# Attention with strided heads first and local heads in turn, expert 0 in three equal token groups, and its first low halves on GpSimd

## The chip, the cores and the metric

The program runs on one core of a Trainium2 chip. The metric is device time in microseconds (us) of one execution; lower is better. The engines are named as in the profile: PE (TensorE matmuls), PEld (TensorE weight loads), DVE (VectorE), ACT (ScalarE), POOL (GpSimd), SP (SyncE, which issues most DMAs).

## The reference, cut to what matters

Three layers follow each other: an attention with two kinds of heads, a mixture of experts with dense Sinkhorn weights, and a second mixture with noisy top-2 routing.

```python
# attention: B, H, S, D = 2, 8, 576, 64
rel = pos[:, None] - pos[None, :]
mask_local = (rel >= 0) & (rel < 32)                       # heads 0..3
mask_strided = (rel >= 0) & (pos[None] % 32 == pos[:, None] % 32)  # heads 4..7
attn = softmax(where(mask, q @ k.T / 8, -1e9)) ; x = attn @ v
# first mixture: N, DM, E, F = 1152, 512, 8, 1024
P = exp(x @ w_gate - max); 8 times: rows and columns of P normalised
out = sum over e of P[:, e] * (relu(x @ w1[e]) @ w2[e])    # every token, every expert
# second mixture: each token goes to its two best experts
```

## The kernel before, in words

Every fp32 product of the mixtures is made as three fp32r matmuls (`mm3`, L162): an operand is split into a high half (an ACT copy that rounds) and a low half (a DVE subtraction), by `split` (L99). `firsts` collects the ACT copies of all such splits in program order; `seen[0]` is the last one.

**Attention** (L170 to L307). `attention(b)` does one batch of 576 tokens in 12 units: two pairs of local heads (hp 0, 1) with three units each (`LOCAL`, three blocks of 64 tokens), then two pairs of strided heads (hp 2, 3) with three units each (`STRIDED`, 4, 4 and 3 groups of residue classes). A local unit covers 192 consecutive tokens; a strided unit covers a set of residues over the whole batch. `unit` (L215) adds the mask and the scores on PE (L220, L225), takes maxima and sums on DVE (L231 to L237), exponentials on ACT (L235), the scaling on POOL (L238), transposes on PE (L241) with a DVE copy (L243, helper L213), and the product with V on PE (L247). The result is split into `xh` and `xl` (128 x 4 x 1152, fp32r), whose second index is the head pair. `hum` (L208) issues matmuls without use, 10 ahead of the first unit's scores and 2 ahead of each of the next 11. Score banks alternate between two PSUM tags ("ad") in the first batch and come from one ("a") in the second.

`load_pair` (L183) issues K, Q and V of a head pair on SP's queue. In the first batch the strided pairs have buffers of their own (`pre`); the local pairs of the first batch and all pairs of the second share K and V buffers two deep (`apool`, tags ks and vs). `load_first` issues the first batch's loads in pair order.

**Expert 0** (L597 to L639) runs in four slices q of 256 hidden units. `pair1` makes h = relu(x w1) for given groups of tokens, `pair2` the product with w2 for one tile of 128 tokens (unscaled, since P isn't known yet). The first loop takes the tokens of `early` (0 to 511, tiles 0 to 3) for q = 0..3; the second loop takes `late` (512 to 1151 in two groups of 320, tiles 4 to 8) for q = 3..0. A slice's weights are fetched with `fetch_u` (1 MB on SP, two buffers) and split by `conv_u1` and `conv_u2`; in the first loop `issue_after` places their ACT copies behind those of unit 9 (q = 0) or unit 12 (q = 1..3) of the first batch. Between the loops stand the gate logits and the Sinkhorn steps (L314 to L353), and `sums` (L617) prepares sums of token quarters on DVE for the experts 1 to 6.

The order on each engine is laid out ahead of time by a planner from dependences, program order and its own cost estimates; `issue_after(i)` puts the instructions that a block issues on i's engine behind i. From expert 7 on the order is written out by hand. Every engine runs its own list in order.

Of the kernel before, what the change touches and what calls it, by code (L numbers as in the profile page):

```python
# [20 lines left out]
STRIDE = 32  # L21
# [41 lines left out]
def tile_kernel(ctx: ExitStack, tc: tile.TileContext, qL, kL, vL, qS, kS, vS, wg, u12, w1, w2, wgn, noise, v1, v2, cst, masks, dummy, out):  # L63
# [32 lines left out]

    seen, firsts = [None], []

    def split(hi, lo, src, relu=False):  # L99
        if relu:  # L100
            seen[0] = nc.scalar.activation(hi, src, AF.Relu)  # L101
            nc.vector.scalar_tensor_tensor(lo, src, 0.0, hi.bitcast(F32), op0=ALU.max, op1=ALU.subtract)  # L102
# [37 lines left out]

    def conv_u1(raw):
        hi, lo = (upool.tile([128, 7, 2, 128], F32R, tag=t, name=t) for t in ("u1h", "u1l"))
        v = raw.rearrange("p c (j n) -> p j c n", j=2)
        for j in range(2):
            split(hi[:, 2 * j:2 * j + 2].rearrange("p a b n -> p (a b) n"),
                  lo[:, 2 * j:2 * j + 2].rearrange("p a b n -> p (a b) n"), v[:, j])
        return [[[x[:, 2 * j + c // 2, c % 2] for c in range(NC)] for j in range(2)] for x in (hi, lo)]
# [32 lines left out]
    flip = [0, 0]  # L180
    where = [0, "ad"]

    def load_pair(b, hp):  # L183
        local = hp < 2
        nq, nk, nb, q, k, v = (NQ, LK, NJ, qL, kL, vL) if local else (GK, GK, NG, qS, kS, vS)
        hp %= 2
        flip[1] = (flip[1] + 1) % 4
        qs = acc[:, 4:].rearrange("p t d -> p (t d)")[:, flip[1] * 640:flip[1] * 640 + nb * nq]
# [5 lines left out]
        else:  # L194
            ks = apool.tile([128, S + STRIDE], F32, tag="ks", name="ks")
            vs = apool.tile([128, NG, 128], F32, tag="vs", name="vs")
        if b == 0 and hp == 0 and local:
            cut = 3 * nq
            nc.sync.dma_start(ks[:, :224], k[b, hp, :, :224])
            nc.sync.dma_start(qs[:, :cut], q[b, hp, :, :cut])  # L200
            nc.sync.dma_start(ks[:, 224:w], k[b, hp, :, 224:])
# [13 lines left out]
    def unit(w, nk, mask, j0, nb, qs, ks, vs, step):  # L215
        nq = 128
        where[0] += 1
        sc = ps(where[1][where[0] % len(where[1])], "sc")
        hum(sc, 10 if where[0] == 1 else 2 if where[0] <= 12 else 0)
        nc.tensor.matmul(sc[:nq, :nb * nk], identb[:nq, :nq], mask, start=True, stop=False)  # L220
# [30 lines left out]
    def load_first():  # L251
        pairs, queue = [], []
        for hp in range(4):
            got, values = load_pair(0, hp)
            pairs.append(got)
            if queue:
                queue.pop(0)()
            queue.append(values)
        queue.pop()()
        return pairs  # L260

    def attention(b):
        pairs = load_first() if b == 0 else None
        for hp in range(4):
            if pairs:
                got = pairs[hp]
            else:
                got, values = load_pair(b, hp)
                values()
            if hp < 2:  # L270
                for j0, nb in LOCAL:
                    first = maskb[:, M_ML:M_MS].rearrange("p (b k) -> p b k", b=3)
                    mask = first if j0 == 0 else first[:, 1:2].to_broadcast([128, nb, LK])
                    ot = unit(NQ, LK, mask, j0, nb, *got, NQ)
                    o = slice(b * S + j0 * NQ, b * S + (j0 + nb) * NQ)
                    split(xh[:, hp, o], xl[:, hp, o], ot[:, :nb * NQ])
            else:
                view = [x[:, hp, b * S:(b + 1) * S].rearrange("p (i r) -> p r i", r=STRIDE) for x in (xh, xl)]
                for j0, nb in STRIDED:
                    mask = maskb[:, None, M_MS:].to_broadcast([128, nb, GK])  # L280
                    ot = unit(GK, GK, mask, j0, nb, *got, GK)
                    r0, r1 = j0 * GR, min((j0 + nb) * GR, STRIDE)
                    split(view[0][:, r0:r1], view[1][:, r0:r1],
                          ot[:, :(r1 - r0) * NI].rearrange("p (r i) -> p r i", i=NI))

# [18 lines left out]
    for j in (64, 96):  # L304
        nc.gpsimd.tensor_tensor(fold2, fold2, ident[:, j:j + 2 * E], op=ALU.add)
    where[1] = "a"
    attention(1)  # L307
# [259 lines left out]
    whole = ((0, 384), (384, 384), (768, 384))  # L567
    early = ((0, 512),)
    late = ((512, 320), (832, 320))

# [26 lines left out]
    for q in range(NP):  # L597
        raw = fetch_u(0, q)
        with tc.issue_after(firsts[min(q, 1) * 3 + 8].ins):
            a, b = conv_u1(raw[0]), conv_u2(raw[1])  # L600
        pair1(a, early)
        for t in range(4):
            pair2(b, t, None, q == 0)
# [25 lines left out]
    for q in range(NP):  # L629
# [521 lines left out]
```

## Time and profile before

| | |
|---|---|
| median of 3 runs | 1119.98 us (1112.18 to 1121.66) |
| the profiled execution, device time | 1110.57 us |
| its span, first to last instruction | 1108.8 us |
| granted TensorE clock, mean | 0.997 |
| PE, PEld, DVE, ACT, POOL busy | 98%, 86%, 60%, 36%, 16% |

Most views are of the profiled execution. A busy PE is not a PE at its peak: matmuls overlap and their ends are modelled, so the distance from start to start tells more than a matmul's own duration. In a row of groups the number after the bar is busy time and the mean duration of one in ns; "idle before" is the engine's idle time ahead of the group and what ended it. An arrow reads "waited for".

### The profile page before, as it was taken

The page shows a single profiled execution, that of the slowest core. Times are in us where ns is not written, and L with a number is a line of the kernel's source. Part 1 is how long each engine was busy: PE and PEld are TensorE (multiplying, and loading weights), DVE is VectorE, ACT ScalarE, POOL GpSimd, SP SyncE. Part 2 cuts the span into 40 slices and gives each one's busy share as a digit, 9 for nine tenths or more (in the row PEclk, how much of TensorE's full clock was granted, in tenths as well). Part 3 has the DMA queues.
Part 4 walks back from the last instruction along what each step waited for, and adds up shares of the span by engine and source line. Part 5 has one row for each costly group of instructions (what it writes and reads, how often), then busy time and mean ns, then how long its engine had stood idle before and what let it go on. Part 6 is the DMA issues. An engine that isn't in the chain of part 4 may idle for free.

```text
span 1108.8 us, 17357 instructions
## 1 busy us (share of the span) xinstructions
PE 1091.7 (98%) x6878; PEld 954.6 (86%) x6878; DVE 664.3 (60%) x1374; ACT 394.4 (36%) x884; POOL 173.2 (16%) x204
## 2 busy tenths in 40 slices
PE   9999999999999999999999999999999999999996
PEld 5677989999899999889999899998888798888885
DVE  5876696666666666666665766554266464445440
ACT  5642335333322333323332333231123254445541
POOL 2210112111111111111111110000040531322211
PEclk9999999999999999999999999999999999999998
DMA  9512143111111121111111111022122673665541
GB/s 277 163 51 76 39 138 126 38 64 52 39 39 38 39 77 39 39 38 39 44 72 39 38 39 41 36 76 76 38 58 86 175 264 101 205 204 203 184 99 23
DMA packets 31425, 97.36 MB, mean 88 GB/s; under 512 B 6486, under 2 KB 15190, under 8 KB 22764
## 3 DMA queue, kind: packets, MB, share of 16 engines
q1 hardware_dynamic: 16028, 78.13, 20.6%
q0 software_dynamic: 5408, 11.26, 4.8%
q10 hardware_dynamic: 9904, 6.83, 2.0%
q8 instruction: 55, 0.90, 0.3%
q14 instruction: 30, 0.25, 0.1%
HBM read 84.69 MB, written 11.60 MB: 87 GB/s over the span
## 4 chain that ended last, share of the span: by engine, by line
PE 87%; DVE 3%; issue 3%; DMA 3%; POOL 2%; ACT 1%; POOLq 0%; ACTq 0%; SPq 0%
PE y L164 40%; PE h L164 16%; PE a L665 14%; PE b L665 7%; PE d L665 3%; PE y L838 2%; DMA table<-en,si 1%; POOL table L498 1%; PE sc L210 1%; PE sc L225 1%; PE tr L241 1%; PE xgt L750 1%; DMA wg_sb<-in_wg 1%; PE ot L247 1%; DMA xg<-x2d,tt 1%
## 5 line engine op out<-in xcount | busy, mean ns | idle before, releaser
L591 DVE SCALAR_TENSOR_TENSOR acc<-y,P,acc 128x512 f32<-128x512 f32 x207 | 152.8, 748 | 141.6 <-PE y L164 141.6
L164 PE MATMUL y<-u2h,gh 128*128 128x512 f32 x504 | 198.6, 394 | 0.5 <-DVE acc L591 0.3
L164 PE MATMUL y<-u2l,gh 128*128 128x512 f32 x504 | 197.3, 391 | 0.0
L164 PE MATMUL y<-u2h,gl 128*128 128x512 f32 x504 | 190.0, 392 | 0.7 <-DVE gl L102 0.6
L154 POOL TENSOR_TENSOR ut<-raw 128x256 f32<-128x256 f32 x48 | 35.0, 750 | 513.7 <-DVE u1l L106 442.6
L164 PEld LDWEIGHTS y<-u2h,gl 128*128 128x128 f32 x504 | 94.4, 188 | 20.8 <-DVE gl L102 2.0
L164 PE MATMUL h<-xh,wh 128*128 128x384 f32 (+8 forms) x352 | 110.8, 315 | 0.3 <-DVE hl L102 0.3
L164 PE MATMUL h<-xl,wh 128*128 128x384 f32 (+8 forms) x352 | 110.4, 314 | 0.1
L164 PE MATMUL h<-xh,wl 128*128 128x384 f32 (+8 forms) x352 | 109.9, 312 | 0.0
L164 PEld LDWEIGHTS y<-u2h,gh 128*128 128x128 f32 x504 | 94.8, 188 | 15.6 <-issue 0.7
L164 PEld LDWEIGHTS y<-u2l,gh 128*128 128x128 f32 x504 | 94.7, 188 | 13.8
L101 ACT ACTIVATE hh<-h 128x256 fp32r<-128x256 f32 (+2 forms) x88 | 35.6, 414 | 101.5 <-PE h L164 101.4
L164 PEld LDWEIGHTS h<-xh,wh 128*128 128x128 f32 x352 | 66.4, 189 | 2.0 <-DVE hl L102 0.6
L164 PEld LDWEIGHTS h<-xl,wh 128*128 128x128 f32 x352 | 66.4, 189 | 1.4 <-issue 0.6
L104 ACT ACTIVATE u2h<-raw 128x1024 fp32r<-128x1024 f32 x31 | 32.9, 1060 | 96.4 <-PE y L164 96.4
L164 PEld LDWEIGHTS h<-xh,wl 128*128 128x128 f32 x352 | 66.4, 189 | 0.0
L102 DVE SCALAR_TENSOR_TENSOR hl<-h,hh 128x256 fp32r<-128x256 f32 (+2 forms) x88 | 40.4, 465 | 40.1 <-ACT hh L101 40.0
L106 DVE TENSOR_TENSOR wl<-raw,wh 128x1024 fp32r<-128x1024 f32 x42 | 49.5, 1222 | 21.4 <-ACT wh L104 21.4
L665 PE MATMUL b<-sh,u1h 128*128 128x288 f32 x192 | 57.0, 297 | 0.0
L665 PE MATMUL a<-sh,u1l 128*128 128x288 f32 x192 | 56.9, 296 | 0.0
L665 PE MATMUL b<-sl,u1h 128*128 128x288 f32 x192 | 56.9, 296 | 0.0
L665 PE MATMUL a<-sl,u1h 128*128 128x288 f32 x192 | 56.8, 296 | 0.0
(248 smaller groups left out, 2487.2 us busy)
## 6 DMA issues: line engine op xcount, KB each, us to landing
raw<-in_u SPq DMA_DIRECT2D x31, 1024.0 KB, 4.8
raw<-in_v SPq DMA_DIRECT2D x20, 1024.0 KB, 9.8
acc<-in_v SPq DMA_DIRECT2D x12, 1024.0 KB, 7.6
raw<-in_w SPq DMA_DIRECT2D x4, 1024.0 KB, 5.0
out<-zero ACTq DMA_DIRECT2D x1, 3072.0 KB, 18.9
x2d<-acc ACTq DMA_DIRECT2D x9, 256.0 KB, 2.0
vs<-in_vL SPq DMA_DIRECT2D x4, 432.0 KB, 10.0
ks<-in_kS SPq DMA_DIRECT2D x4, 297.0 KB, 7.6
```

The source lines that it names most:

```text
L101: seen[0] = nc.scalar.activation(hi, src, AF.Relu)
L102: nc.vector.scalar_tensor_tensor(lo, src, 0.0, hi.bitcast(F32), op0=ALU.max, op1=ALU.subtract)
L104: seen[0] = nc.scalar.activation(hi, src, AF.Copy)
L106: nc.vector.tensor_tensor(lo, src, hi.bitcast(F32), op=ALU.subtract)
L154: nc.gpsimd.tensor_tensor(t[:, o], x, y, op=ALU.subtract)
L164: nc.tensor.matmul(o, a, b, start=start, stop=stop)
L210: nc.tensor.matmul(o, onesb, onesb[:, None, :].to_broadcast([128, 4, 128]), start=True, stop=True)
L225: nc.tensor.matmul(sc[h * 64:h * 64 + w, i * nk:(i + 1) * nk], qs[r, j * w:(j + 1) * w], ks[r, j * step:j * step + nk], start=False, stop= ...
L241: nc.tensor.transpose(tr[:nk, i * nq:(i + 1) * nq], s[:, i], ident[:nq, :nq])
L591: nc.vector.scalar_tensor_tensor(acc[:, t], p, P[:, t, scale:scale + 1], acc[:, t], op0=ALU.mult, op1=ALU.add)
L665: nc.tensor.matmul(p, l[:, b, c], m, start=first and i == 0, stop=i == 5, skip_group_check=not first)
L838: nc.tensor.matmul(p[j * w:j * w + k, :d], hr[:, f, :k], raws[f // 4][:, f % 4, j * d:(j + 1) * d], start=f == 0, stop=f == 7)
```

## The change

- In both batches the strided pairs (hp 2, 3) come first; then the local units alternate between the pairs 0 and 1, block by block. The first batch's loads go in the order 2, 3, 0, 1, and the load that is cut in two is now pair 2's.
- Useless matmuls stand ahead of the first 10 units (`BUSY`), and the score banks come from tag "a" alone from unit 11 on.
- Expert 0 takes tokens 0 to 383 (tiles 0 to 2) in the first loop, and two groups of 384 (tiles 3 to 8) in the second.
- The ACT copies of the weights are placed behind unit 7's (q = 0) and unit 10's (q = 1..3).
- The low half of w1's first slice (q = 0) is made by four GpSimd subtractions instead of two on DVE.
- The DVE instructions of `sums` stand behind the first relu's low half.

```diff
 def split(hi, lo, src, relu=False):
     if relu:
-            nc.vector.scalar_tensor_tensor(lo, src, 0.0, hi.bitcast(F32), ...)
+            lows.append(nc.vector.scalar_tensor_tensor(lo, src, 0.0, hi.bitcast(F32), ...))
...
-    def conv_u1(raw):
+    def conv_u1(raw, pool=False):
...
         for j in range(2):
+            if pool:
+                h = hi[:, 2 * j:2 * j + 2].rearrange("p a b n -> p (a b) n")
+                nc.scalar.activation(h, v[:, j], AF.Copy)
+                for a in range(2):
+                    nc.gpsimd.tensor_tensor(lo[:, 2 * j + a], v[:, j, 2 * a:2 * a + 2], hi[:, 2 * j + a].bitcast(F32),
+                                            op=ALU.subtract)
+                continue
...
+    BUSY = 2 * len(STRIDED) + 2 * (len(LOCAL) - 1)
...
-        flip[1] = (flip[1] + 1) % 4
+        if b > 0 or local:
+            flip[1] = (flip[1] + 1) % 4
...
-        if b == 0 and hp == 0 and local:
-            cut = 3 * nq
-            nc.sync.dma_start(ks[:, :224], k[b, hp, :, :224])
+        if b == 0 and hp == 0 and not local:
+            cut = STRIDED[0][1] * GK
+            nc.sync.dma_start(ks[:, :cut], k[b, hp, :, :cut])
...
-        hum(sc, 10 if where[0] == 1 else 2 if where[0] <= 12 else 0)
+        hum(sc, 10 if where[0] == 1 else 2 if where[0] <= BUSY else 0)
...
-        for hp in range(4):
-            got, values = load_pair(0, hp)
+        for hp in (2, 3, 0, 1):
+            pairs[hp], values = load_pair(0, hp)
...
+        for hp in (2, 3):
+            for j0, nb in STRIDED:
+                strided_unit(b, hp, j0, nb, get(hp))
+        for j0, nb in LOCAL:
+            if where[0] == BUSY:
+                where[1] = "a"
+            for hp in (0, 1):
+                local_unit(b, hp, j0, nb, get(hp))
...
-    where[1] = "a"
     attention(1)
...
-    early = ((0, 512),)
-    late = ((512, 320), (832, 320))
+    early = whole[:1]
+    late = whole[1:]
...
-        with tc.issue_after(firsts[min(q, 1) * 3 + 8].ins):
-            a, b = conv_u1(raw[0]), conv_u2(raw[1])
+        with tc.issue_after(firsts[min(q, 1) * 3 + 6].ins):
+            a, b = conv_u1(raw[0], q == 0), conv_u2(raw[1])
         pair1(a, early)
-        for t in range(4):
+        for t in range(3):
...
-        for t in range(4, NT):
+        for t in range(3, NT):
...
-    with tc.issue_after(marks[1]):
+    with tc.issue_after(marks[1]), tc.issue_after(lows[0].ins):
         sums()
```

`whole` is ((0, 384), (384, 384), (768, 384)). `get(hp)` loads a pair of the second batch when its first unit asks for it.

## Rows read from the trace of the kernel before

**Rows 1.** Busy time by stretch: us, then PE, PEld, DVE, ACT, POOL, clock, DMA.

```profile
0.00:7.30 7.30, 6.17 (x20) 2.42 (x20) 0.00 (x0) 1.28 (x1) 1.83 (x14) 1.00 0.72 206
7.30:33.70 26.40, 26.17 (x412) 18.64 (x411) 20.48 (x76) 17.83 (x98) 7.08 (x12) 1.00 0.99 279
33.70:83.10 49.40, 47.11 (x467) 34.69 (x464) 38.88 (x103) 25.81 (x104) 9.32 (x17) 1.00 0.29 96
...
110.80:166.00 55.20, 54.43 (x310) 49.14 (x309) 45.14 (x108) 19.30 (x36) 8.04 (x8) 1.00 0.28 88
```

**Rows 2.** One of these stretches, the useless matmuls of line 210 alone (PE, PEld).

```profile
7.30:33.70 26.40, 4.80 (x16) 1.23 (x16) 1.00 0.99 279
```

**Rows 3.** Timeline of PE, 27 to 44 us: start, length, instruction, idle before.

```profile
27.85 0.71 PE L225 MATMUL sc<-ks,acc 64*64 64x96 f32 x12
...
33.75 0.50 PE L164 MATMUL h<-xh,u1h 128*128 128x512 f32 x1
...
38.77 0.53 PE L241 MATMUL tr<-cs,s 128*96 128x128 f32 x3 [0.56 <-POOL s L238]
...
43.12 0.74 PE L164 MATMUL h<-xh,u1h 128*128 128x512 f32 x2
```

**Rows 4.** Timeline of DVE, splits of attention results: units 9, 12, last of batch 2.

```profile
31.73 0.40 DVE L106 TENSOR_TENSOR xl<-ot,xh 128x144 fp32r<-128x144 f32 x1
...
42.20 0.41 DVE L106 TENSOR_TENSOR xl<-ot,xh 128x144 fp32r<-128x144 f32 x1
...
80.46 0.43 DVE L106 TENSOR_TENSOR xl<-ot,xh 128x144 fp32r<-128x144 f32 x1 [1.82 <-ACT xh L104]
```

**Rows 5.** The chain that ended last, in order of time: start, us, matmuls back to back.

```profile
83.28 5.37 PE h L164 x23
...
163.37 1.76 PE h L164 x12
...
736.12 7.97 PE h L164 x46
```

**Rows 6.** Busy time by stretch, matmuls of line 164 alone (PE, PEld).

```profile
33.70:83.10 49.40, 25.91 (x96) 17.21 (x97) 1.00 0.29 96
```

**Rows 7.** Groups of DVE instructions from 7.3 to 33.7 us.

```profile
L622 DVE TENSOR_TENSOR r<-xh,xl 128x576 f32<-128x576 f32 x2 | 1.5, 755 | 0.0
```

**Rows 8.** Instructions on the tile raw, to 60 us: duration min/median/max, first and last start.

```profile
L104 ACT ACTIVATE u1h<-raw x6: 617/620/633, 32.3 to 46.1; 128x512 fp32r<-128x512 f32 x6
L106 DVE TENSOR_TENSOR u1l<-raw,u1h x6: 656/680/685, 33.3 to 48.0; 128x512 fp32r<-128x512 f32 x6
```

**Rows 9.** Groups of POOL subtractions from 130 to 170 us.

```profile
L154 POOL TENSOR_TENSOR ut<-raw,ut 128x256 f32<-128x256 f32 x4 | 4.8, 1189 | 0.2
L154 POOL TENSOR_TENSOR ut<-raw 128x256 f32<-128x256 f32 x4 | 3.4, 862 | 77.6 <-DMA raw<-in_u 60.3 <-DVE u1l L106 17.3
```

**Rows 10.** Timelines of DVE and of POOL where the two overlap.

```profile
14.41 0.15 DVE L236 TENSOR_SCALAR sm<-sm 128x3 f32<-128x3 f32 x1
...
15.33 0.52 DVE L236 TENSOR_SCALAR sm<-sm 128x3 f32<-128x3 f32 x1 [0.20 <-ACT s L235]
...
15.15 0.67 POOL L238 TENSOR_TENSOR s<-s,sm 128x288 f32<-128x288 f32 x1 [1.14 <-DVE nmx L232]
...
47.66 1.52 POOL L238 TENSOR_TENSOR s<-s,sm 128x288 f32<-128x288 f32 x1 [6.01 <-DVE nmx L231]
```

**Rows 11.** Groups of POOL instructions from 30 to 40 us: the wait for a constant.

```profile
L300 POOL CAST upper<-cs 128x128 bf16<-128x128 f32 x1 | 0.3, 291 | 6.6 <-DMA cs<-in_cst 6.6
```

**Rows 12.** Timeline of SP's queue: loads of the second batch's first pairs.

```profile
11.71 0.35 SPq L204 DMA_DIRECT2D ks<-in_kL  x1
...
33.41 0.35 SPq L204 DMA_DIRECT2D ks<-in_kS  x1
```

**Rows 13.** DMA issues to 60 us: KB each, median us from issue to landing.

```profile
vs<-in_vL SPq DMA_DIRECT2D x4, 432.0 KB, 10.0
ks<-in_kS SPq DMA_DIRECT2D x4, 297.0 KB, 7.6
```

More of the change, by code (lines that the diff above doesn't have):

```diff
@@ L95, in tile_kernel @@
     P = cpool.tile([128, NT, E], F32, name="P")
-    seen, firsts = [None], []
+    seen, firsts, lows = [None], [], []
     def split(hi, lo, src, relu=False):
@@ L101, in split @@
             seen[0] = nc.scalar.activation(hi, src, AF.Relu)
-            nc.vector.scalar_tensor_tensor(lo, src, 0.0, hi.bitcast(F32), op0=ALU.max, op1=ALU.subtract)
+            lows.append(nc.vector.scalar_tensor_tensor(lo, src, 0.0, hi.bitcast(F32), op0=ALU.max, op1=ALU.subtract))
         else:
@@ L196, in load_pair @@
             vs = apool.tile([128, NG, 128], F32, tag="vs", name="vs")
-        if b == 0 and hp == 0 and local:
-            cut = 3 * nq
-            nc.sync.dma_start(ks[:, :224], k[b, hp, :, :224])
+        if b == 0 and hp == 0 and not local:
+            cut = STRIDED[0][1] * GK
+            nc.sync.dma_start(ks[:, :cut], k[b, hp, :, :cut])
             nc.sync.dma_start(qs[:, :cut], q[b, hp, :, :cut])
-            nc.sync.dma_start(ks[:, 224:w], k[b, hp, :, 224:])
+            nc.sync.dma_start(ks[:, cut:w], k[b, hp, :, cut:])
             nc.sync.dma_start(qs[:, cut:], q[b, hp, :, cut:])
@@ L251, in load_first @@
     def load_first():
-        pairs, queue = [], []
-        for hp in range(4):
-            got, values = load_pair(0, hp)
-            pairs.append(got)
+        pairs, queue = {}, []
+        for hp in (2, 3, 0, 1):
+            pairs[hp], values = load_pair(0, hp)
             if queue:
@@ L260, in load_first @@
         return pairs
-    def attention(b):
[L263 to L268, printed above, removed]
-                values()
[L270 to L284, printed above, removed]
@@ new lines, in local_unit, with strided_unit @@
+    def local_unit(b, hp, j0, nb, got):
+        first = maskb[:, M_ML:M_MS].rearrange("p (b k) -> p b k", b=3)
+        mask = first if j0 == 0 else first[:, 1:2].to_broadcast([128, nb, LK])
+        ot = unit(NQ, LK, mask, j0, nb, *got, NQ)
+        o = slice(b * S + j0 * NQ, b * S + (j0 + nb) * NQ)
+        split(xh[:, hp, o], xl[:, hp, o], ot[:, :nb * NQ])
+    def strided_unit(b, hp, j0, nb, got):
+        view = [x[:, hp, b * S:(b + 1) * S].rearrange("p (i r) -> p r i", r=STRIDE) for x in (xh, xl)]
+        mask = maskb[:, None, M_MS:].to_broadcast([128, nb, GK])
+        ot = unit(GK, GK, mask, j0, nb, *got, GK)
+        r0, r1 = j0 * GR, min((j0 + nb) * GR, STRIDE)
+        split(view[0][:, r0:r1], view[1][:, r0:r1],
+              ot[:, :(r1 - r0) * NI].rearrange("p (r i) -> p r i", i=NI))
@@ new lines, in attention, with get @@
+    def attention(b):
+        pairs = load_first() if b == 0 else {}
+        def get(hp):
+            if hp not in pairs:
+                pairs[hp], values = load_pair(b, hp)
+                values()
+            return pairs[hp]
+        for hp in (2, 3):
[6 more added lines that the diff above has]
+                local_unit(b, hp, j0, nb, get(hp))
```

## The prediction

> **What bounds the kernel now.** I read the busy time by stretch first, because the change touches only the first 166 us of a span of 1108.8 us. In the stretch from 7.3 to 33.7 us, the first batch's attention, PE is busy 26.17 of 26.40 us [rows 1]; DVE, with 20.48 us, and ACT, with 17.83 us, have room. So PE sets the pace there, though 16 of its matmuls are the useless ones [rows 2]. From 33.7 to 83.1 us the second batch's attention and half of expert 0's first loop share PE: 47.11 of 49.40 us, 2.3 us idle. From 110.8 to 166 us PE idles 0.8 us. Those and 0.2 us of the first batch, 3.3 us, are all the idle time that I can find in what the change touches; the granted clock is 1.00 in each of these stretches.
>
> Second, the PE timeline around the seam [rows 3]. Expert 0's first product runs at 33.75 us. It doesn't wait for the whole first batch: unit 9's low half is written from 31.73 us, and unit 12's only from 42.20 us [rows 4]. PE starts on the head pairs that are ready, and the product that resumes at 43.12 us is one that needed unit 12. Ahead of 33.75 us PE also runs scores of the second batch, from 27.85 us on (the first of three such groups), because its K was loaded early. So the seam is already filled with work of other stages.
>
> Third, the chain that ended last, for the price of a product in a run without gaps: 5.37/23 = 0.233 us with 512 columns, 1.76/12 = 0.147 us with 320, and 7.97/46 = 0.173 us with 384 [rows 5].
>
> **The change part by part.**
>
> *Useless matmuls.* There are 10 + 11 x 2 = 32 before and 10 + 9 x 2 = 28 after. Four fewer are worth 4 x 0.233 = 0.9 us if PE sets the pace, and nothing if another engine does. With PE busy in 26.17 of 26.40 us [rows 1] I take 0.9.
>
> *Three equal groups.* Each slice q has 24 products for each group of tokens. Before: 24 x (0.233 + 2 x 0.147) = 12.65 us; after: 24 x 3 x 0.173 = 12.46 us. That is 0.2 us for each of four slices, together 0.7 us with the unrounded prices [rows 5]. The second product has nine tiles either way. Of the splits behind the first product there are three for each half slice either way. I take 0.7; the lower bound is 0, if the 384 rate doesn't hold here, where DVE is busier.
>
> *Order of the heads, and the earlier start of expert 0.* Units, instructions and loads are the same in number. All heads have tokens 0 to 383 after unit 10 instead of 12, so no part of expert 0's first product has to wait as the one at 43.12 us did [rows 3]. But PE isn't idle in the time that this saves: what starts sooner pushes back work that has to be done as well. It is worth the idle time that it fills. Of the 3.3 us, the gap of 0.56 us ahead of 38.77 us [rows 3] has a cause that I can name: POOL waits 6.6 us for a constant that ACT's queue loads behind unit 9 [rows 11], and with it the first scaling of the second batch. After the change unit 9 keeps its place in the order, but the second batch reaches POOL later, so this wait should hold up less. I take 1.0 us; the bounds are 0 and 3.3.
>
> *Low halves on GpSimd.* Two DVE subtractions of 0.68 us leave DVE, 1.4 us [rows 8]; POOL gets four of 128x256. The same shape takes POOL 0.862 or 1.189 us on average in another stage [rows 9], so 3.4 to 4.8 us, for a POOL that is busy 7.08 of 26.40 us [rows 1]. Its cover is the time from unit 7's ACT copy to unit 10's split, three units: nine units were through from 7.3 to 31.73 us [rows 4], 2.7 us each, so some 8 us. The weights must have landed, and ACT's copies are 0.62 us each [rows 8]. What queues behind them on POOL is the scaling of units 8 to 10; if none is covered, the start is 3.4 to 4.8 us later, and PE has the last units' matmuls to fill most of that. Moreover POOL slows DVE: a DVE instruction of 0.15 us took 0.52 us while POOL worked on its scaling, and a POOL scaling of 0.67 us took 1.52 us elsewhere [rows 10]. At 0.37 us for each of four, DVE loses up to 1.5 us, about what it is given. As PE sets the pace, I book a cost of 0.2 us; the bounds are 0 and 1.5.
>
> The Trainium skill ("SBUF — State Buffer", section "SBUF: two separate sides") states that VectorE and GpSimd share a pair of SBUF ports under an exclusive lock: whichever starts first holds it for its whole instruction, and the other blocks fully. The trace agrees in kind: 0.15 to 0.52 us in rows 10. By that rule each subtraction could hold DVE for its whole length, 3.4 us or more in all, and the move would cost DVE 2 us net instead of nothing; with PE as the pacer most of that would still be hidden, and the sum would be about 1 us smaller.
>
> *Sums behind the first relu.* Two subtractions of 0.755 us leave DVE's list ahead of 33.7 us [rows 7] and come back in the next stretch, where DVE has 10.5 us free [rows 1]. Nothing is booked; without that room it is 1.5 us of DVE.
>
> *Loads.* K and V of the second batch share two buffers with the first batch's local pairs. Before, those pairs ran first, and the second batch's first K was issued at 11.71 us; the one for its third pair was issued at 33.41 us [rows 12]. After, both buffers stay in use to units 11 and 12, so no K of the second batch is issued much ahead of 27 us, and V later still. A load takes 7.6 to 10.0 us to land [rows 13]. The second batch's pair 1 waits in the same way for pair 3's last unit. The scores from 27.85 us then come after 33 us. PE has expert 0's first loop to run meanwhile, so what it costs are short waits of an order laid out ahead: I book 0.2 us, with bounds of 0 and several us (the second rival). The weights' loads of 1 MB stand on the same SP queue and can only come sooner, since fewer loads precede them.
>
> *Cover.* The first loop is shorter: four slices were 4 x 48 x 0.233 = 44.8 us, and are 4 x (24 x 0.173 + 18 x 0.233) = 33.4 us. By 83.1 us, 96 products or 22.4 us of it had been used [rows 6], just after the second batch's last split at 80.46 us [rows 4]. So 11.0 us of cover are left where 22.4 us were. That costs nothing as long as the second batch isn't 11 us later.
>
> *Sum.* 0.9 + 0.7 + 1.0 - 0.2 - 0.2 = 2.2 us. The span goes from 1108.8 to 1106.6 us. The profiled execution took 1110.57 us, 9.4 us below the median of the runs, 1119.98 us; against that median it is 1117.8 us.
>
> **The rivals.**
>
> *Nothing comes.* The 1.6 us of the first two terms are eaten by new short waits of the planner's order, or the four matmuls were free. For it: PE is full on both sides of the seam, and the whole scope is a few us. 1120 us, give or take 0.5.
>
> *Slower: the second batch starves.* Place: SP's loads of K and V at lines 204 and 206 behind units 11 and 12, and pair 1's behind pair 3. One load is 7.6 to 10.0 us [rows 13], two in a row 15 to 20 us. It decides when the second batch's last split comes over 11.0 us later than 80.46 - 2.2, that is past 89 us; every us beyond is a us of empty PE. A slip of 16 us gives +5 us, 1125; it takes 22 us of slip for +11. For it: two waits where there were none. Against it: DVE and ACT have room to catch up, and the weights' half of the work needs none of these loads.
>
> *The whole scope.* All 3.3 us of idle time go, the start moves so that the 16 useless matmuls of [rows 2] (16 x 0.233 = 3.7 us) cost nothing more, and the groups give 0.7 us: 7.7 us, 1112.3. Against it: 12 of the 16 remain in the program.
>
> **How the numbers follow.** The forecast, a gain of 0.5 to 5 us (1115 to 1119.5), has a chance of 0.5; nothing 0.2; the slower rival 0.2, of it 0.05 beyond 11.2 us; the whole scope 0.1, of it 0.02 beyond. One per cent, 11.2 us, is about what a measurement of this kernel can tell from no change, and its own three runs lie 9.5 us apart. For that spread I add 0.04 on the faster side and 0.03 on the slower: faster 0.06, same 0.86, slower 0.08. The range goes from the lowest run less 7.7 us (1112.18, so 1105) to the highest plus 5 us (1121.66, so 1127); both terms are needed, as any case may meet any run.
>
> **What would show it.** In the changed kernel's trace: 28 useless matmuls; the first product of expert 0 at 31 to 33 us, with 384 columns at 0.173 us, and no break for the local pairs after it; idle time of PE from there to 83 us near 1.5 instead of 2.3 us; four POOL subtractions ended ahead of the first product that reads them; K of the second batch issued after 25 us; its last split ahead of 89 us, with first-loop products still left after it. I am wrong if PE sits idle behind a K or V load or behind those four subtractions, if the clock falls, or if the Sinkhorn steps end too late for expert 1.

## The result: 6 us slower, where 2 us faster was forecast

| | kernel before | changed kernel |
|---|---|---|
| median of the runs beside each other | 1116.19 us (20 runs) | 1120.88 us (20 runs) |
| ratio of the times | | 1.0055, interval 1.0033 to 1.0076 |
| the ratio, measured again | | 1.0057, interval 1.0033 to 1.0081 |
| span of the profiled execution | 1108.8 us | 1116.9 us |

The change costs about 6 us, and the interval excludes a gain. The time lies in the range and within the one per cent that the forecast called the likeliest, but that range was made wide by the spread of the runs, and a loss of 6 us fits into it as well as a gain. The sign is wrong. Two of the 20 runs of the kernel before took 2752 and 3786 us; the ratio is of the fast runs and leaves them out, the median doesn't.

Busy time of the changed kernel in the stretches of [rows 1], and in one more, in which the Sinkhorn steps end. The columns are us, then PE, PEld, DVE, ACT and POOL, granted clock, DMA share, GB/s.

```profile
7.30:33.70 26.40, 23.12 (x388) 16.73 (x386) 19.76 (x72) 19.46 (x101) 10.41 (x16) 1.00 0.88 254
33.70:83.10 49.40, 47.43 (x469) 37.37 (x466) 36.34 (x99) 25.96 (x103) 13.47 (x18) 0.93 0.41 130
110.80:166.00 55.20, 55.20 (x283) 50.51 (x282) 44.94 (x103) 18.08 (x32) 7.62 (x8) 1.00 0.36 110
166.00:190.00 24.00, 22.07 (x127) 19.64 (x126) 18.07 (x48) 8.87 (x20) 2.87 (x4) 0.93 0.29 97
```

The last stretch in the kernel before:

```profile
166.00:190.00 24.00, 24.00 (x151) 22.15 (x150) 18.47 (x36) 12.86 (x26) 6.75 (x8) 1.00 0.46 148
```

In this pair of executions two columns matter. PE's idle time in the four stretches was 0.2, 2.3, 0.8 and 0 us before and is 3.3, 2.0, 0 and 1.9 us now: 3.9 us more. And the granted clock was 1.00 in all four. Now it is 0.93 in the second and in the fourth, and 0.07 of 49.4 and of 24 us is 3.5 and 1.7 us of TensorE's full speed. Together that is 9.1 us, or 8.2 if the four useless matmuls that are gone are worth their 0.9 us. The spans differ by 8.1 us.

The first copy that is scaled by the finished P shows how much of it has come by then. First the kernel before, then the changed one (ACT's timeline: start, length, instruction):

```profile
181.04 0.66 ACT L588 ACTIVATE y<-y,P 128x512 f32<-128x512 f32 x1 [0.29 <-PE y L164]
```

```profile
188.17 1.24 ACT L604 ACTIVATE y<-y,P 128x512 f32<-128x512 f32 x2 [1.44 <-PE y L171]
```

So 7.1 of the 8.1 us are lost ahead of 188 us. There are three places. Here is PE's timeline at each:

```profile
15.96 0.29 PE L229 MATMUL sc<-mask_sb 128*128 128x288 bf16 x1
17.78 0.71 PE L234 MATMUL sc<-ks,acc 64*64 64x96 f32 x12 [1.53 <-DMA acc<-in_qL]
...
40.38 0.57 PE L256 MATMUL ot<-at,vs 96*64 96x64 f32 x12
42.92 1.05 PE L250 MATMUL tr<-cs,s 128*54 128x128 f32 x4 [1.97 <-POOL s L247]
...
178.68 0.39 PE L364 MATMUL cs<-c,onesr 128*128 128x8 f32 x2 [1.51 <-DVE c L362]
```

At 16 us PE waits 1.5 us for the queries of the second local pair. At 41 us it waits 2.0 us for a scaling on GpSimd. At 177 us it waits 1.5 us for the last Sinkhorn step. In this execution the clock falls behind the second and the third pause, and not behind the first. These are the stretches of 2 us around the two:

```profile
39.00:41.00 2.00, 1.94 (x34) 1.48 (x31) 2.00 (x5) 1.36 (x4) 2.00 (x1) 1.00 1.00 294
41.00:43.00 2.00, 0.08 (x1) 0.09 (x2) 1.92 (x5) 0.42 (x2) 2.00 (x2) 0.97 0.87 325
43.00:45.00 2.00, 2.00 (x17) 1.23 (x19) 0.99 (x3) 0.00 (x0) 0.28 (x1) 0.50 0.55 169
45.00:47.00 2.00, 2.00 (x16) 1.61 (x13) 0.62 (x3) 0.00 (x0) 0.00 (x0) 0.50 0.10 32
47.00:49.00 2.00, 2.00 (x20) 1.25 (x19) 0.00 (x0) 0.00 (x0) 0.00 (x0) 0.50 0.01 3
...
178.00:180.00 2.00, 1.32 (x8) 1.33 (x9) 1.33 (x7) 0.00 (x0) 0.00 (x0) 0.85 0.38 160
180.00:182.00 2.00, 2.00 (x10) 2.00 (x9) 0.47 (x1) 0.63 (x2) 0.00 (x0) 0.50 0.00 0
182.00:184.00 2.00, 2.00 (x14) 2.00 (x14) 0.93 (x2) 0.52 (x3) 0.00 (x0) 0.79 0.00 0
```

From 43 to 49 us TensorE is granted the lower of its two levels, 1.2 GHz, while it is busy all the time. PE's busy column does not show this: it reads 2.00 of 2.00.

The pause at 41 us has its cause in the timelines of POOL and DVE:

```profile
39.00 4.28 POOL L247 TENSOR_TENSOR s<-s,sm 128x216 f32<-128x216 f32 x2 [3.04 <-DVE sm L246]
```

```profile
38.75 0.52 DVE L102 SCALAR_TENSOR_TENSOR gl<-h,gh 128x384 fp32r<-128x384 f32 x1
39.19 1.41 DVE L638 TENSOR_TENSOR r<-xh,xl 128x576 f32<-128x576 f32 x2
40.53 0.16 DVE L245 TENSOR_SCALAR sm<-sm 128x3 f32<-128x3 f32 x1
40.60 0.59 DVE L222 COPY at<-tr 54x432 f32<-54x432 f32 x1
41.11 0.67 DVE L106 TENSOR_TENSOR u1l<-raw,u1h 128x512 fp32r<-128x512 f32 x1
41.71 0.16 DVE L246 RECIPROCAL sm<-sm 128x3 f32<-128x3 f32 x1
41.80 0.66 DVE L106 TENSOR_TENSOR u1l<-raw,u1h 128x512 fp32r<-128x512 f32 x1
42.37 0.55 DVE L102 SCALAR_TENSOR_TENSOR gl<-h,gh 128x384 fp32r<-128x384 f32 x1
```

Two scalings stand in the first row. The first of them, of 216 columns, begins at 39.00 us and ends only at 42.9 us; elsewhere one takes 0.55 us. In those 3.9 us DVE works through a closed row of eight instructions: two sums, two low halves of u1, a low half of g at the end, and between them the small steps and a copy. The two sums at 39.19 us are the ones that the change put behind the first relu. In the kernel before they ran one at a time and earlier:

```profile
21.68 0.76 DVE L622 TENSOR_TENSOR r<-xh,xl 128x576 f32<-128x576 f32 x1
...
32.57 0.75 DVE L622 TENSOR_TENSOR r<-xh,xl 128x576 f32<-128x576 f32 x1
```

So the reading of the trace gives one theory: **the held scaling** (theory H). The later sums close DVE's row, DVE's row holds the scaling on GpSimd, PE pauses for the scaling, and the clock falls behind the pause. The other theories on trial were the Sinkhorn stall at 177 us by itself, the loads of the second batch, the late queries of the second local pair, and the smaller group of tokens.

### The profile page after: what moved, and what is told of

The parts are those of the page before. It is cut to its first block, busy times and chain, and to the rows that moved or that the text cites. A ratio compares the mean times of both kernels' runs of the same rounds, so it can differ in the third digit from the quotient of the medians.

```text
span 1116.9 us, 17360 instructions
## 1 busy us (share of the span) xinstructions
PE 1094.6 (98%) x6874; PEld 961.9 (86%) x6874; DVE 663.6 (59%) x1372; ACT 394.4 (35%) x884; POOL 179.2 (16%) x208
## 4 chain that ended last, share of the span: by engine, by line
PE 88%; issue 3%; DMA 3%; DVE 3%; POOL 1%; ACT 1%; another core or an unknown queue 0%; SPq 0%; POOLq 0%; DVEq 0%; ACTq 0%
PE y L171 41%; PE h L171 16%; PE a L681 13%; PE b L681 7%; PE d L681 3%; PE y L854 2%; DMA acc<-in_qL 1%; PE ot L256 1%; PE sc L234 1%; PE tr L250 1%; PE xgt L766 1%; DVE wl L106 1%; DMA table<-en,si 1%; DMA xg<-x2d,tt 1%; POOL table L514 0%
## 5 line engine op out<-in xcount | busy, mean ns | idle before, releaser
L681 PE MATMUL b<-sh,u1l 128*128 128x288 f32 x192 | 57.2, 298 | 0.0
```

The costliest lines, as they stand in the source:

```text
L681: nc.tensor.matmul(p, l[:, b, c], m, start=first and i == 0, stop=i == 5, skip_group_check=not first)
```

## The experiments

Each ratio is to the runs of the kernel before on the same chip, with its 95% interval. A ratio of 0.001 is 1.1 us. Single executions of one kernel differ by 10 us and more, so the verdicts rest on the ratios (12 runs of each kernel, 6 of the one with more buffers, 20 behind the first table), and a profile shows only the mechanism in one of them.

### Half of the Sinkhorn steps, in both kernels

```diff
-        for _ in range(8):
+        for _ in range(4):
```

> The changed kernel with 4 Sinkhorn iterations instead of 8 (it leaves half of that computation out). Theory A, the late Sinkhorn end costs the time: P ended at 179.7 us (last L369) in the changed kernel and at 169.9 us (last L353) before, PE then waited 1.5 us at 176.8 us and ran at half clock around 182 us, and 4.8 us of the profile's 8.2 us fall between 166 and 186 us. With 4 iterations P ends before 150 us, the wait and the low clock go, and this kernel is within 2.5 us of its counterpart b_sink4. Rival B, the loss is made in the second batch's attention (33 to 85 us) and only carried on: it stays 5 to 6 us behind b_sink4.

> The kernel before with the same 4 Sinkhorn iterations (half of that computation left out), as the counterpart. Both theories: 0 to 2 us faster than the kernel before, since its PE hardly waited for the Sinkhorn steps (P ended at 169.9 us, first used at 181.0 us), and DVE is full from 140 to 160 us.

Measured: 1.0036 (1.0018 to 1.0054) for the changed kernel with four steps, 1.0008 (0.9986 to 1.0029) for the one before. The difference between the two kernels is 0.0028 instead of 0.0055. The stall at 177 us is gone with the late steps, and about half of the loss would go with it; but the intervals are as wide as this half, so it is not settled. Some loss seems to be left when no Sinkhorn step is late. The expectation's two theories said under 2.5 us or 5 to 6; the 3 us measured decide for neither.

### The sums not held behind the first relu

```diff
-    with tc.issue_after(marks[1]), tc.issue_after(lows[0].ins):
+    with tc.issue_after(marks[1]):
```

> The changed kernel without the gate that puts the sums' DVE instructions behind the first relu. Theory C: the gate drops two 0.7 us subtractions of two SBUF inputs (L638, 39.2 us) and the next weights' low halves in a row in front of the second batch's first scalings; two POOL scalings took 4.28 us from 39.0 us, PE waited 1.97 us for them and its clock fell to half from 43 to 49 us. Without it the scalings take 0.55 us each again, PE's gap at 41 us is under 0.6 us, no half clock before 60 us, the second batch's last split comes at 80 to 82 us instead of 85.0, and the kernel is 2 to 6 us faster than the changed one (ratio to before 1.000 to 1.004). Rival: the gate only moves work that DVE has to do anyway; ratio 1.004 to 1.007.

Measured: 1.0010 (0.9992 to 1.0028), so 5 us of the 6 come back. The sums run at 28.64 and at 50.08 us, far from each other; the scaling takes 0.55 us; and PE has no pause at the last Sinkhorn step. But three signs of the expectation failed in the profile: PE still pauses 1.34 us at 39 us (for an exponential), the last split comes at 85.97 us, and there is half clock before 60 us. Most of that half clock stands behind another pause, the one for the late queries, which is 3.03 us long here:

```profile
20.82 1.23 PE L234 MATMUL sc<-ks,acc 64*64 64x96 f32 x12 [3.03 <-DMA acc<-in_qL]
...
22.00:30.00 8.00, 8.00 (x64) 4.89 (x64) 4.16 (x12) 2.37 (x10) 0.67 (x1) 0.50 0.41 156
```

So the time came back, and the clock, in this execution, didn't.

### More buffers for K and V of the second batch

```diff
-            ks = apool.tile([128, S + STRIDE], F32, tag="ks", name="ks")
-            vs = apool.tile([128, NG, 128], F32, tag="vs", name="vs")
+            ks = apool.tile([128, S + STRIDE], F32, tag="ks", name="ks", bufs=4)
+            vs = apool.tile([128, NG, 128], F32, tag="vs", name="vs", bufs=4)
```

> The changed kernel with K and V buffers four deep instead of two, so that the second batch's loads wait for no unit of the first. Theory D, the prediction's slower rival: the held loads delay the second batch; its K is then issued before 22 us, its last split comes 2 to 4 us sooner than 85.0 us and the kernel is 2 to 5 us faster than the changed one. Theories A and C: no PE wait of the changed kernel's second batch names one of these loads, so the same within 1.5 us (ratio 1.004 to 1.007).

Measured: 1.0073 (1.0055 to 1.0090). Loads that no longer wait for a buffer bring nothing. The run is no clean test, though: the loads of K and V that are free to go stand ahead of expert 0's weights on the same queue, so the first weights are issued at 19.36 instead of 12.80 us, and the last split comes at 90.62 instead of 85.0 us. What speaks against the forecast's slower rival, the starving second batch, is the trace of the changed kernel itself: its last split comes ahead of the 89 us that the rival needed. The run shows one thing more: no scaling is held in its profile (none takes over 1.47 us), and it is the slowest kernel of all.

### The hold on the sums alone, in the kernel before

```diff
...
-    with tc.issue_after(marks[1]):
+    with tc.issue_after(marks[1]), tc.issue_after(lows[0].ins):
```

The lines left out collect `lows` in `split`, as in the change.

> The kernel before with one line of the change alone: the sums of the Winograd weights wait for the first relu's low half. Theory G (the gate by itself sets the loss): the first two pairs of sums leave 21.7 and 32.6 us and come behind about 38 us, the sums that follow and the Sinkhorn steps come later (P's last step at 175 to 180 instead of 169.9), and the time is 4 to 6 us over the kernel before, ratio 1.004 to 1.005. Rival R (the gate costs only in the order that the rest of the change makes, where strided heads come first and the local pairs alternate): the last step of P stays ahead of 174 us and the ratio is 1.000 +- 0.002. A third outcome, the prediction's booking (nothing, since VectorE has room behind the first relu), gives the same as R and differs from it only in that the gate would cost nothing in the changed kernel either, which the run without it has already excluded.

Measured: 1.0012 (0.9988 to 1.0037). The hold by itself doesn't cost the 6 us: in the order of the kernel before, the sums go to 47.0 us, and no scaling stands in their way there. Theory G, 4 to 6 us, fails, and its rival R came: the line costs what it costs only together with the rest.

### The first loads in another order

```diff
-            if queue:
+            if hp == 3:
                 queue.pop(0)()
             queue.append(values)
-        queue.pop()()
+        for values in queue:
+            values()
```

This puts K and Q of the second local pair ahead of V of the second strided and of the first local pair. It was run alone and without the hold on the sums.

> The changed kernel with the first loads in another order: keys and queries of the second local pair ahead of the values of the second strided pair. Theory Q (the 1.5 us in which TensorE waits at 16 us for the queries of the second local pair is lost for good): that gap shrinks to under 0.5 us, and the time is 1 to 2 us less than the changed kernel's, ratio to the kernel before 1.004 (from 1.0055). Rival (the gap is repaid by later waits, as the second batch is held by its own chain, or the values of the second strided pair become the late ones at 19 us): ratio 1.0055 +- 0.0015 with the gap gone or moved.

> The changed kernel without the gate on the sums and with the first loads reordered as in the other run. If the gate (5 us) and the late queries (1 to 2 us) are separate losses, 1.0010 falls to 0.9995 or less, 1113 us where the kernel before takes 1113.4: the two would then hold the whole loss. If the late queries cost nothing, it stays at 1.001 +- 0.0015.

Measured: 1.0000 (0.9978 to 1.0022) alone, and 0.9980 (0.9963 to 0.9996) without the hold on the sums. The pause for the queries at 16 us is gone in both. It was expected to be worth 1 to 2 us; the loads gave 6. So the theory of the late queries is right in that they cost, and wrong in the amount; most of the difference goes with the clock, as the means of all runs show behind the last experiment. In the profile of the first, the two sums stand in the same row of DVE, at 37.68 us, and the scaling slips in between:

```profile
37.48 0.55 POOL L247 TENSOR_TENSOR s<-s,sm 128x216 f32<-128x216 f32 x1 [3.04 <-DVE sm L246]
```

```profile
37.24 0.52 DVE L102 SCALAR_TENSOR_TENSOR gl<-h,gh 128x384 fp32r<-128x384 f32 x1
37.68 1.63 DVE L639 TENSOR_TENSOR r<-xh,xl 128x576 f32<-128x576 f32 x2
```

Here the two sums take 1.63 us instead of 1.41: DVE waited 0.2 us, not GpSimd 3.3. PE then has no idle time at all from 33.7 to 83.1 us, at a clock of 1.00:

```profile
33.70:83.10 49.40, 49.40 (x495) 39.38 (x495) 40.71 (x104) 25.27 (x102) 8.93 (x12) 1.00 0.37 127
```

### Groups of 384 tokens

In the kernel before, alone, and taken back in the changed kernel:

```diff
-    early = ((0, 512),)
-    late = ((512, 320), (832, 320))
+    early = whole[:1]
+    late = whole[1:]
...
```

The lines left out move the two loops over tiles from `range(4)` and `range(4, NT)` to 3.

> The kernel before with expert 0 in three groups of 384 tokens instead of 512, 320 and 320, and nothing else of the change. The prediction's booking: 0.7 us gained from the faster columns at 384, ratio 0.9994. Rival C (cover): the work that may fill TensorE beside the second batch's attention is a group of 384 tokens instead of 512, a quarter less, so TensorE runs dry between 33 and 85 us, the last split comes 2 to 5 us later than 80.5 us, and the time is 2 to 4 us more, ratio 1.002 to 1.004.

> The changed kernel with expert 0's groups of 512, 320 and 320 tokens as before. If the groups of 384 bring 0.7 us, as the prediction booked, the ratio rises to 1.006; in the kernel before they moved it by 0.0007 +- 0.002. Rival C (with 384 tokens there is less work to put beside the second batch's attention, and the Sinkhorn steps get the order whose last step stalls TensorE by 1.5 us, as in the kernel before with these groups alone): the stall at 177 us goes and the ratio falls by 0.002 to 0.005.

Measured: 1.0007 (0.9987 to 1.0028) with the new groups in the kernel before, 1.0038 (1.0014 to 1.0061) with the old ones in the changed kernel. Neither shows a gain of 0.7 us or a loss; both intervals hold either. The stall at 177 us came with the groups of 384 in the profile of the first, and went with the old groups in that of the second, but the times didn't follow it. The profile of the first is a warning against reading one execution: PE pauses 2.88 us for a scaling at 40 us, the clock is 0.50 from 42 to 50 us and falls again at 180 us, and this execution took 1120.19 us, 7 us over the median of its kernel, which on the whole loses nothing.

### The pauses filled with useless work

```diff
...
-            p = ps("b", "cs")
+            p = ps("b", "cs"); hum(p, 7 if k == 7 else 0)
```

The line left out names the loop's counter `k`.

> The changed kernel with seven useless matmuls of 512 columns ahead of the product of the last Sinkhorn step: 7 x 0.213 = 1.5 us of work put where TensorE paused 1.5 us for VectorE at 176.8 us and the granted clock then fell to 0.50 between 180 and 182. Clock theory: the pause is filled, the clock stays at 1.00 from 166 to 190, and the time falls by the half-speed stretch, 1.5 to 3 us, ratio 1.003 to 1.004 (from 1.0055), though TensorE does more. Rival (the lateness itself is what costs, not the clock): the work only stands where the pause stood, ratio 1.0055 +- 0.0015; if VectorE is later still behind it, up to 1.007.

```diff
-        tr = ps("b", "tr")
+        tr = ps("b", "tr"); hum(tr, 8 if where[0] == 13 else 0)
```

> The changed kernel with eight useless matmuls of 512 columns (1.7 us) ahead of the transposes of the second batch's first unit, where TensorE paused 2.0 us at 40.7 us for GpSimd's scaling and then ran at 0.50 from 43 to 49 us. Clock theory: the granted clock from 43 to 49 us stays at 1.00, worth about 3 us, of which the useless matmuls may take back up to 1.7: ratio 1.0025 to 1.0045. Rival (GpSimd's scaling, stretched to 3.9 us by VectorE, holds the second batch whatever TensorE does): the last split stays at 85 us and the ratio at 1.0055 or above.

Measured: 1.0042 (1.0016 to 1.0068) with the Sinkhorn pause filled, 1.0026 (1.0007 to 1.0044) with the one at 41 us filled. The second gives back 3 us (0.0029, uncertain by as much) though TensorE has 1.7 us more to do. Its profile shows no pause for the transposes, the useless matmuls in their place, and the clock at 1.00 from 33 to 60 us:

```profile
39.32 0.49 PE L250 MATMUL tr<-cs,s 128*96 128x128 f32 x3
39.64 1.89 PE L219 MATMUL tr<-onesb 128*128 128x512 bf16 x8
41.37 0.60 PE L250 MATMUL tr<-cs,s 128*54 128x128 f32 x4
```

That is the clock theory's outcome, with two reservations: the planner moved DVE's instructions too, and the scaling took 2.0 us instead of 3.9; and the profile has half clock elsewhere, from 11 to 14 us behind a pause of 1.96 us for other queries, and around 180 us. The filler at the Sinkhorn step can't be told from no effect.

### The first low halves back on VectorE

```diff
-        a, b = conv_u1(raw[0], q == 0), conv_u2(raw[1])
+        a, b = conv_u1(raw[0]), conv_u2(raw[1])
```

> The changed kernel with the four first low halves of expert 0 back on VectorE (two subtractions of 512 columns). The prediction's booking: GpSimd's four cost 0.2 us, so nothing that can be measured, ratio 1.0055 +- 0.0015. Rival (the four subtractions on GpSimd, 3.9 us in all at 29.7 us, hold back the scalings of the units that are in flight, or by the order they bring set up the 2-us pause at 41 us): the pause goes and the ratio falls to 1.003 or below.

Measured: 1.0010 (0.9986 to 1.0033). This is the rival's outcome: 5 us come back, and PE's pause at 41 us is gone, though DVE's row is still there and a scaling at 41.35 us takes 1.49 us. PE doesn't wait for it in this order.

### The one scaling moved to VectorE, and two kernels measured again

```diff
-        nc.gpsimd.tensor_tensor(s, s, sm[:nq, :nb, None].to_broadcast([nq, nb, nk]), op=ALU.mult)
+        (nc.vector if where[0] == 14 else nc.gpsimd).tensor_tensor(
+            s, s, sm[:nq, :nb, None].to_broadcast([nq, nb, nk]), op=ALU.mult)
```

> The changed kernel with one scaling, that of the second batch's second unit, moved from GpSimd to VectorE: the one that took 3.9 us instead of 0.55 at 39 us. Theory H (this held scaling sets the loss: a 2.0-us pause of TensorE and then 6 us at half the clock): the pause at 41 us and the half clock from 43 to 49 go, and the ratio falls to 1.000 to 1.002. Rival (the hold is a symptom; a late second batch and the Sinkhorn stall at 177 us set it): ratio 1.004 or above with the pause gone.

> The changed kernel itself, a second look. If the hold belongs to the kernel: a scaling of about 3.9 us at 38 to 40 us, a pause of TensorE of 2.0 us behind it, ratio 1.0055 +- 0.0015. If it comes and goes: the scaling at 0.55 us in this look and times spread over 10 us or more, ratio 1.003 to 1.006.

> The changed kernel with the first loads reordered, a second look. If the hold belongs to the timing of the kernel: the scaling at 37.5 us takes 0.55 us again, TensorE does not pause for it, and the ratio is 1.000 +- 0.002 again. If it comes and goes: the profile may show a scaling of 3 to 4 us at 37 us and a half-clock stretch, and the ratio lies between 1.000 and 1.004.

Measured: 1.0019 (0.9995 to 1.0042) with the scaling of unit 14 on VectorE, beside 1.0057 (1.0033 to 1.0081) for the changed kernel itself on the same chip. The pause and the half clock from 43 to 49 us are gone in its profile, and 4 us come back (0.0038, with the two intervals taken together 0.0034 either way). That is the ratio that theory H named. The scaling takes 0.37 us on VectorE. But this execution has half clock in another place. It pauses 1.94 us for the late queries, and the clock is 0.50 for 12 us behind that:

```profile
17.69 1.00 PE L234 MATMUL sc<-ks,acc 64*64 64x96 f32 x12 [1.94 <-DMA acc<-in_qL]
...
18.00:30.00 12.00, 12.00 (x114) 8.45 (x111) 5.33 (x18) 4.42 (x17) 2.00 (x3) 0.50 0.54 198
```

The two repeats add two things. The hold belongs to the changed kernel: its second profile has the same 4.28 us and the same pause of 1.97 us. But the clock doesn't always fall behind it:

```profile
41.00:43.00 2.00, 1.13 (x13) 0.76 (x15) 1.34 (x3) 0.00 (x0) 1.23 (x2) 1.00 0.68 253
43.00:45.00 2.00, 2.00 (x29) 1.44 (x29) 1.05 (x5) 0.00 (x0) 0.00 (x0) 1.00 0.18 51
45.00:47.00 2.00, 2.00 (x25) 1.72 (x20) 1.10 (x3) 1.53 (x9) 0.00 (x0) 1.00 0.00 0
```

In this execution the first copy scaled by P comes at 183.19 us instead of 188.17: 5 us, between two executions of one kernel whose pauses for the scaling and for the last Sinkhorn step are the same and whose clock is not. The clock's share of the first one, 3.5 and 1.7 us, is as much.

The kernel with reordered loads gave 0.9999 (0.9984 to 1.0014) again, but this time its profile has the hold:

```profile
39.19 4.27 POOL L247 TENSOR_TENSOR s<-s,sm 128x216 f32<-128x216 f32 x2 [3.72 <-DVE sm L246]
```

with the pause of 1.97 us and a clock of 0.67 and 0.50 from 43 to 47 us. This profiled execution took 1117.72 us, 4 us over the median of its own runs. So there the hold comes and goes. How often it comes, the profiles can't tell, and so they can't tell how much of the loads' 6 us is the hold that is missed.

### Several undoings at once

> The changed kernel without the gate on the sums, with the first loads reordered, and with the first low halves of expert 0 back on VectorE. If each of the three only removes the same loss, nothing is left to remove: ratio 0.998 +- 0.002 as with the first two. If the low halves on GpSimd cost something of their own, it falls to 0.996; if they were worth their 0.2 us or more, it comes to 0.999 or above.

> The changed kernel without the gate and with the first loads reordered, a second look. If it is below the kernel before: ratio 0.998 +- 0.0015 again, and no pause over 1 us at 175 us for the Sinkhorn steps. If the first look was the luck of its runs: 0.9995 or above.

> The changed kernel with the first loads reordered and the scaling of the second batch's second unit on VectorE. If the hold still costs something in the part of the runs that have it: ratio 0.997 to 0.999 (from 1.000 with the loads alone). If the reordered loads have already taken the whole loss, or if the order that the planner makes with the moved scaling is no better: 1.000 +- 0.0015 or above.

Measured: without the hold on the sums and with reordered loads, 0.9980 (0.9963 to 0.9996) and measured again 0.9989 (0.9971 to 1.0008). With the low halves back on VectorE as well, 0.9990 (0.9970 to 1.0010). With the loads reordered and unit 14's scaling on VectorE, 0.9987 (0.9969 to 1.0005). All lie 1 to 2 us below the kernel before, and only the first interval excludes 1, so none is shown to beat it. The three undoings don't add up: alone they take 0.0045, 0.0055 and 0.0045 off the ratio of 1.0055, together 0.0065. So in part they take away the same loss.

**The granted clock of all runs.** Every run has, beside its time, a mean granted clock, and this settles part of what single profiles leave open. Among the runs of one and the same kernel, 0.001 of the clock goes with about 1.2 us (fitted over the 367 runs of the experiments and of the kernel before beside them; correlation -0.86). These are the means:

| kernel | ratio | clock, its runs | clock, kernel before beside them |
|---|---|---|---|
| changed kernel, measured again | 1.0057 | 0.9917 | 0.9953 |
| sums not held | 1.0010 | 0.9925 | 0.9954 |
| scaling of unit 14 on VectorE | 1.0019 | 0.9921 | 0.9953 |
| useless work at 41 us | 1.0026 | 0.9936 | 0.9946 |
| low halves back on VectorE | 1.0010 | 0.9938 | 0.9946 |
| loads reordered | 1.0000 | 0.9948 | 0.9950 |
| loads reordered, measured again | 0.9999 | 0.9947 | 0.9953 |

The changed kernel's clock is 0.0037 lower (0.0017 either way) than that of the kernel before. By the fit this is worth about 4.5 of its 5.7 us; that is an estimate. The load order goes with the clock throughout: the six sets of runs with the loads reordered have means of 0.9947 to 0.9956, the ten sets of the changed kernel and its variants with its own load order 0.9905 to 0.9938, whether a scaling is held in their profile or not. With the loads reordered no profile has half clock before 30 us. So most of the 6 us that the loads gave back goes with the clock. Theory H is at most half right: with the scaling freed about 4 us come back, but the clock is 0.0004 higher (0.0023 either way), so the runs give no sign that they came by way of the half clock behind its pause.

## Why the prediction was wrong

**Sums behind the first relu: one of two steps that failed.** "Nothing is booked; without that room it is 1.5 us of DVE." The room was there: DVE is idle 13 of 49.4 us from 33.7 to 83.1. The step priced DVE's own time and didn't ask which other instructions the two sums would come to stand beside. They closed a row of 4 us on DVE, and GpSimd's scaling had to get through in that time. Leaving out the hold gives back 5 us, moving the scaling 4 us, each uncertain by 3 to 4 us; PE's pause for the scaling is 2 us. The rows for it had been read: a scaling of 0.67 us that took 1.52 us [rows 10]. The prediction used them for the other direction alone, GpSimd slowing DVE.

**Low halves on GpSimd: size right, effect missed.** The four took 3.9 us (forecast 3.4 to 4.8) and ended at 33.6 us, ahead of the first product that reads them at 34.5:

```profile
29.69 3.93 POOL L149 TENSOR_TENSOR u1l<-raw,u1h 128x256 fp32r<-128x256 f32 x4
```

A booking of 0.2 us is too small for the runs to confirm. Yet back on VectorE 5 of the 6 us are gone. In its profile the planner has laid out another order, in which PE doesn't wait for a scaling; that this is the reason isn't shown.

**Useless matmuls: 0.9 us that didn't come.** They are 28, and TensorE is busy 3 us less up to 33.7 us, but the time went into waiting, of it 1.5 us for the late queries. "PE sets the pace there" was read off a busy time of which the useless matmuls were a part. How much of the waiting the four had covered isn't shown, as no run puts them back.

**Loads: the other step that failed; the wrong ones were priced.** K of the second batch is issued at 25.8 and 27.6 us, as forecast, and the last split comes at 85.0 us, ahead of 89. But "loads are the same in number" skipped the first batch: the last pair to be loaded was needed from unit 10 before and from unit 8 now, since the local pairs alternate. That is the 1.5 us at 16 us, in no term of the sum. Reordering them takes back all 6 us, twice. The clock's mean rises from 0.9917 to 0.9947 with it, 3.7 us by the fit, and the pause of 1.5 us would make up most of the rest.

**The clock: a term that was missing.** The forecast read 1.00 in every stretch and named a falling clock only as a sign of being wrong. The sum carried no price for it. By the runs it is the largest part of the loss, about 4.5 us.

**Groups of 384: not measured.** The first loop's products run at 0.173 us as priced:

```profile
37.14 0.34 PE L171 MATMUL h<-xl,u1h 128*128 128x384 f32 x1
37.31 0.34 PE L171 MATMUL h<-xh,u1l 128*128 128x384 f32 x1
37.49 0.34 PE L171 MATMUL h<-xl,u1h 128*128 128x384 f32 x1
```

Their 0.7 us is smaller than what the runs can tell.

**Idle time: 1.0 us booked, 0.3 us found.** The first product of expert 0 runs at 32.35 us, and POOL no longer waits 6.6 us for its constant. From 33.7 to 83.1 us the idle time is 1.97 instead of 2.29 us. But it now lies in one piece, and in this execution a clock of 0.93 behind it costs more than ten times what was saved.

**Cover: right.** From 83.1 to 110 us TensorE doesn't run dry; it is busy all of the 26.9 us.

**Sinkhorn: named as a danger, without a price.** The last step of P goes from 169.87 to 179.75 us, and PE stalls 1.5 us for it. The same stall stands in the profiles of kernels that lose nothing (reordered loads, low halves on VectorE), so the stall alone isn't the loss. What the half clock behind it costs on the whole stays open.

What is shown, then: the loss doesn't belong to one edit. Reordering the loads takes it all back, and leaving out the hold or freeing the one scaling takes back 4 to 5 of the 6 us, with an uncertainty of 3 to 4. Most of the loss goes with a lower granted clock, and the clock comes back with the reordered loads. What is argued: that the pause for the late queries is what sets off the low clock. The two profiles with 8 and 12 us of half clock right behind it speak for it; against it stands that the same pause cost no clock in the two profiles of the changed kernel itself. What is open: whether freeing the scaling is worth more than its pause of 2 us, the share of the Sinkhorn stall, why a pause costs clock in some executions and not in others, and why the scaling is held in one execution of the kernel with reordered loads and not in the other.

## What to carry to other kernels

Price a moved instruction by what it will stand beside, not only by its own time: DVE with a quarter of its time free can still have a closed row of 4 us in which a short GpSimd step on the critical path is held. Ask of every short step that another engine waits for which long row could cover it, and take the busy column of TensorE with the granted clock beside it. Where a planner lays out the order, undo each part alone before blaming one: here three different undoings each gave back 5 to 6 of 6 us. Before one profile is explained, put the mean clock of all runs beside their times: here it pointed to the first loads, where the profile of the changed kernel pointed to the scaling.

## What was not expected of the hardware

- A GpSimd instruction of 0.55 us took 3.9 us beside a row of eight DVE instructions, and ended about with the last of them. The Trainium skill ("SBUF — State Buffer", section "SBUF: two separate sides") says that the holder of the shared port pair has it for its whole instruction and the other blocks. That covers a wait for one instruction of DVE. Here the scaling lasted through the whole row, in which a copy of 0.59 us and small steps stood too. The same was seen in four other profiles. In another kernel's execution with nearly the same row (reordered loads) it got through at once, and DVE paid 0.2 us.
- TensorE's answer to the same pause differs. After a pause of 1.97 us the granted clock was 0.50 for 6 us in one execution of the changed kernel and 1.00 throughout in the other. After a pause of 1.5 us at the last Sinkhorn step it was 0.50 from 180 to 182 us in the one, and in the other it stayed at 1.00:

```profile
174.00:176.00 2.00, 1.25 (x9) 1.25 (x10) 1.35 (x7) 0.00 (x0) 0.00 (x0) 1.00 0.48 201
176.00:178.00 2.00, 1.80 (x14) 1.56 (x13) 0.99 (x3) 0.82 (x2) 0.00 (x0) 1.00 0.00 0
```

- So one profile of a kernel like this may lie 5 to 7 us beside its median: 1114.18 beside 1118.99 us for the changed kernel measured again, 1120.19 beside 1113.17 us for the groups of 384. The clock in the profile shows most of the cause.
